# When the sums' rows and the products enter the sync queue: a change to a fused attention and gated-MLP kernel

## The chip, the cores and the metric

The kernel runs on one core of a Trainium2 chip. The core has a matrix engine (TensorE, PE in the rows; its weight loads are PEld), a vector engine (VectorE, DVE), a scalar engine (ScalarE, ACT), a general engine (GpSimd, POOL) and a sync engine (SyncE, SP), which here only issues transfers. Each engine runs its own instructions in the order in which they stand, and engines wait for each other by semaphores. Sixteen DMA engines move the data. The metric is the device time of one execution in microseconds; lower is better.

## The reference

Attention with an added relative bias, then a gated layer on the heads' joined outputs:

```python
scores = q @ k.T / 8 + bias            # 4 batches, 8 heads, 576 x 576, head size 64
attn   = exp(scores - max); attn = attn / (sum(attn) + 1e-9)
x      = (attn @ v) joined over heads  # 2304 tokens x 512
out    = (sigmoid(x @ w_gate) * (x @ w_val)) @ w_out     # 512 -> 1536 -> 512
```

The bias comes from a small two-layer net on log-distances and is the same for all batches.

## The kernel before, in words

**Stages.** The bias stage runs to about 111 us of the profiled span, attention from there to about 374 us, the gated layer from there to the end.

**Attention** (`attention`, lines 500 to 792) works through 16 units; a unit is one pair of heads of one batch. `n` counts slots, nine to a unit; slot `s` of unit `u` is `n = 9u + s`. Eight slots are blocks of 128 queries of one of the two heads (`TURN` gives head `h` and block `it`), the ninth holds the last 64 queries of both. In the even slots `score` (L633, L622) writes scores of two blocks to PSUM banks of the pool `ps_s`, and `soft` takes the row minimum on VectorE (L649) and the exponential on ScalarE (L654) to the tile `en`, with the row's sum. Two slots later (`LAG`) `turn` transposes the block for the second product and splits it into two half-precision parts in the tile `at`: half of the blocks on TensorE (L678, L685, then L563 and L564), the other half, the **crossed tiles** of turn slots 1, 3, 5 and 7 (`CROSS`; all of the second head, blocks 0 to 3), on GpSimd (L531, L672, tile `cr`) and then by one transposing DMA from `cr` to `at` (L673). These four DMAs of a unit are called **T1, T3, T5 and T7** here. They are put on the list `crossed` with the slot in which they are due, two after the turn: slot 5, slot 7, and slots 0 and 2 of the next unit.

**The second product** (`products`, L729) of unit `u - 1` runs in slots 3, 5, 7 of unit `u` and slot 1 of unit `u + 1`, 14 matmuls each time. Its first half (`e = 0`, slots 3 and 5) covers the first 288 queries, so it reads what T1, T3 and T5 bring; the second (`e = 1`) reads what T5 and T7 bring. Each half leaves the one accumulator bank (`ps_v`) by a ScalarE copy to `xe` (L733). After the second one, `xe` is written to memory (`xs`, L735).

**The sums.** At slot 3 `tail` of the unit before transposes its last 64 queries and its sums' inverses (`normal`, L698); in slot 4 ScalarE copies those to `rt` (L702), and two small DMAs write them to the rows `rs` (L704, L705).

**The order on the sync queue** is that of the code: within a slot first `after`, then `due` (loads of k, q and v for later units: `kr` L542 due at slot 2, `qr` L548 at slot 5, `vr` L553 at slot 1), then `softs` and `late` (here the `rs` rows), then the due crossed tiles, then the matmuls of `products` (here `xs`, in slot 1), then `extra`. A DMA that must wait for its data holds up all that stand behind it on the queue. The load `qr` waits until GpSimd has read the q before it (`prep_q`, slot 4), `kr` likewise (`prep_k`, slot 1).

**From unit 12 on** `extra` also starts the gated layer: by the table `PLAN` it loads parts of x (`xin`, L879), the sums' rows (`xrec`, L886) and weights (`ww`, L905), and scales and splits x (L894 to L896). `xin` tiles have three buffers, so a load of one can wait for the split (L896) of an earlier x. After the last unit the gated layer's first matmuls follow on TensorE (L974).

The lines below are the heart of the order; the functions that the change touches are printed after them.

```python
            for f in after:
                f()
            for f in due:
                f()
            for f in softs + late:
                f()
            due, loads = loads, []
            while crossed and (crossed[0][0] <= n or n == 9 * NU + LAG):
                crossed.pop(0)[1]()
```

Of the kernel before, what the change touches and what calls it, by code (L numbers as in the profile page):

```python
# [10 lines left out]
F32 = mybir.dt.float32  # L11
# [7 lines left out]
B, H, S, D = 4, 8, 576, 64  # L19
# [9 lines left out]
LAG, WSTEP, VSTEP, TAIL = 2, 2, (3, 5), 3  # L29
# [487 lines left out]
def attention(tc, att, q, k, v, biases, biasL, ident, xs, rs, sizes, extra):  # L517
# [3 lines left out]
    nc = tc.nc  # L521
# [48 lines left out]
    def prep_k(u):  # L570
        kt[u] = t = two.tile([128, 2, S], F32R, name="k")
        pool_split(t[:, 0], t[:, 1], qkraw[u, "kr"])
# [24 lines left out]
    ps_v = pool("ps_v", 1, space=PSUM)  # L597
    ps_s = pool("ps_s", 2, space=PSUM)
# [14 lines left out]
    def score(n):  # L613
        u, s = divmod(n, 9)
        ks, qs = kt[u], qt[u]
        if s == 0:
            state[u] = [st.tile([128, 9], F32, name="sm"), None, {}]
        if s == 8:
            ps = ps_s.tile([128, 2, 512], F32, name="sc")
            for i, (l, r) in enumerate(TERMS):  # L620
                for e in range(2):
                    nc.tensor.matmul(out=ps[:, e, 0:HF], lhsT=qs[:, l, 512:640], rhs=ks[:, r, HF * e:HF * e + HF],  # L622
                                     start=(i == 0), stop=(i == len(TERMS) - 1))
            return [soft(u, s, ps)]
        if s % 2:
            return []
        it = TURN[s][1]
        pair = [ps_s.tile([128, 2, 512], F32, name="sc") for _ in range(2)]
        for i, (l, r) in enumerate(TERMS):
            for e in range(2):  # L630
                for h in range(2):
                    rows = slice(64 * h, 64 * h + 64)
                    nc.tensor.matmul(out=pair[h][:, e, 0:HF], lhsT=qs[rows, l, 128 * it:128 * it + 128], rhs=ks[rows, r, HF * e:HF * e + HF],  # L633
                                     start=(i == 0), stop=(i == len(TERMS) - 1))
        return [soft(u, s + h, pair[h]) for h in range(2)]
# [22 lines left out]
    def turn(n):  # L658

        u, s = divmod(n, 9)  # L660
        p, b = units[u]
        if s == 0:
            state[u][1] = atp.tile([128, 2, 9, S], F16, name="at")
        sm, at, ens = state[u]
        h, it = TURN[s] if s < 8 else (0, 4)
        en = ens[4 * h + it if s < 8 else 8]
        i = slice(128 * it, 128 * it + 128)
        if s in CROSS:
            t = crp.tile([128, 2 * S], F16, name="cr")
            copy(t[:, 0:S], en)  # L670
            for a, z in ((640, slice(0, 512)), (S, slice(512, S))):
                nc.gpsimd.tensor_tensor(out=t[:, a:a + z.stop - z.start], in0=en[:, z], in1=t[:, z], op=ALU.subtract)  # L672
            crossed.append((n + LAG + XLAG, lambda: nc.sync.dma_start_transpose(out=at[:, h, :, i], in_=t)))  # L673
            return []
        after = []
        pt = ps_t.tile([128, 4, 128], F32, name="pt")
        for J in range(4):
            nc.tensor.transpose(pt[:, J], en[:, 128 * J:128 * J + 128], ident)  # L678
        if s == 8:
            return [split(at[:, h, 0:4, 512:576], at[:, h, 5:9, 512:576], pt[:, :, 64 * h:64 * h + 64]) for h in range(2)]  # L680
        after.append(split(at[:, h, 0:4, i], at[:, h, 5:9, i], pt))
        if it == 3:
            pt = ps_t.tile([128, 4, 128], F32, name="pt")
            for e in range(4):
                nc.tensor.transpose(pt[0:64, e], ens[4 * h + e][:, 512:576], ident)  # L685
            after.append(split(at[0:64, h, 4, 0:512], at[64:128, h, 4, 0:512], pt[0:64].rearrange("p e i -> p (e i)")))
        return after

    def tail(u):
        sm, at, ens = state[u]  # L690
        pt = ps_t.tile([128, 4, 128], F32, name="pt")
        nc.tensor.transpose(pt[0:64, 0], ens[8][:, 512:576], ident)
        last = normal(u, pt)
        return [split(at[0:64, :, 4, 512:576], at[64:128, :, 4, 512:576], pt[0:64, 0].rearrange("p (h i) -> p h i", h=2)), last]

    def normal(u, pt):
        p, b = units[u]
        nc.tensor.transpose(pt[0:9, 2], state[u][0], ident)  # L698
        rt = rtp.tile([9, 128], F32, name="rt")

        def leave():
            nc.scalar.activation(out=rt, in_=pt[0:9, 2], func=AF.Copy, scale=sizes["out"][0:9])  # L702
            to = rs[2 * p:2 * p + 2, S * b:S * b + S]
            nc.sync.dma_start(out=to[:, 0:512].rearrange("h (i p) -> h i p", p=128), in_=rt[0:8])  # L704
            nc.sync.dma_start(out=to[:, 512:576].rearrange("(o h) p -> o h p", o=1), in_=rt[8:9].rearrange("o (h p) -> o h p", h=2))  # L705

        return leave

    def invert(u):
        sm = state[u][0]  # L710

        def both():
            nc.vector.tensor_tensor(out=sm, in0=sm, in1=sizes["tiny"], op=ALU.add)
            nc.vector.reciprocal(out=sm, in_=sm)

        return both

    def products(u):
        p, b = units[u]
        sm, at, ens = state[u]  # L720
        vv = vsplit[u]
        xe = xep.tile([128, S], F32, name="xe")
        for e in range(2):
            cs = slice(HF * e, HF * e + HF)
            acc = ps_v.tile([128, 512], F32, name="acc")
            mms = [(J, z, 5 * y + J) for J in range(4) for z, y in TERMS] + [(4, z, 4) for z in range(2)]
            for i, (J, z, y) in enumerate(mms):
                for h in range(2):
                    nc.tensor.matmul(out=acc[D * h:D * h + D, 0:HF], lhsT=vv[:, h, J, z], rhs=at[:, h, y, cs],  # L729
                                     start=(i == 0), stop=(i == len(mms) - 1))  # L730

                def leave(cs=cs, acc=acc, e=e):
                    nc.scalar.activation(out=xe[:, cs], in_=acc[:, 0:HF], func=AF.Copy)  # L733
                    if e == 1:
                        nc.sync.dma_start(out=xs[128 * p:128 * p + 128, S * b:S * b + S], in_=xe)  # L735

                yield leave if i == len(mms) - 1 else None

    NU = len(units)
    crossed = []  # L740
    with tc.manual_schedule():
        work = iter(())
        after, late, due, loads = [], [], [], []
        for n in range(9 * NU + LAG + 1):
            u, s = divmod(n, 9)
            softs = score(n) if n < 9 * NU else []
            inverse = invert(u - 1) if s == 0 and u > 0 else None
            later = turn(n - LAG) if LAG <= n < 9 * NU + LAG else []
            if s == TAIL and u > 0 or n == 9 * NU + LAG:
                later += tail(u - 1)  # L750
            if s == KSTEP and u + 1 < NU:
                prep_k(u + 1)
                if u + 2 < NU:
                    loads.append(lambda z=u + 2: load_k(z))
            if s == QSTEP and u + 1 < NU:
                prep_q(u + 1)
                if u + 2 < NU:
                    loads.append(lambda z=u + 2: load_q(z))
            for f in after:
                f()  # L760
            for f in due:
                f()
            for f in softs + late:
                f()
            due, loads = loads, []
            while crossed and (crossed[0][0] <= n or n == 9 * NU + LAG):
                crossed.pop(0)[1]()
            after, late = ([], later) if s % 2 else (later, [])
            if inverse:
                inverse()  # L770
            if s == WSTEP and 0 < u < NU:
                work = products(u - 1)
            if n == 9 * NU + LAG - 1:
                work = products(u - 1)
            for _ in range(FILL[s] if n < 9 * NU else 14 if n < 9 * NU + LAG else 0):
                f = next(work, None)
                if f:
                    f()
            if s in VSTEP and u < NU:
                upper_v(u, VSTEP.index(s))  # L780
            if s - 2 in VSTEP and u < NU:
                after.append(lower_v(u, VSTEP.index(s - 2)))
            if s == 8 and u + 1 < NU:
                loads.append(lambda z=u + 1: load_v(z))
            extra(n)
        for f in after + late:
            f()
        for f in work:
            if f:
                f()  # L790


class Moe:
# [551 lines left out]
```

## Time and profile before

| what | value |
|---|---|
| runs | 789.0 us median of 3 (788.83 to 792.26) |
| the profiled execution | 791.89 us, of which the span from first to last instruction 790.1 |
| granted TensorE clock, mean | 0.982 of full speed |
| TensorE busy | 735.1 us, 93% |
| VectorE busy | 631.6 us, 80% |
| ScalarE busy | 549.6 us, 70% |
| GpSimd busy | 326.3 us, 41% |
| data moved by DMA | 112.43 MB, mean 142 GB/s |

Busy time is a sum over the whole span and hides that stages differ, so the stages are read one by one. In the rows "idle before, releaser" tells how long an engine stood still and what ended that; a transfer is named by out<-in (`at<-cr` is a crossed tile's transposing DMA). The sync engine's rows (SPq) are issues: their length is the time in which the queue is taken, not the transfer's.

### The profile page before, as it was taken

What the parts mean: (1) busy time and instruction counts of PE and PEld (TensorE: products, weight loads), DVE (VectorE), ACT (ScalarE), POOL (GpSimd) and SP (SyncE); (2) the same over time, 40 slices, a digit from 0 to 9 for tenths busy, and PEclk for the clock granted to TensorE, in tenths of its full rate; (3) what the DMA queues carried; (4) which work ended last, traced back from release to release, by engine and by line L of the source; (5) the groups of instructions that cost most, each with busy time, mean ns of one, the idle gap of its engine ahead of it and who ended that gap; (6) DMA issues with size and microseconds to landing.
All of it is one profiled execution on the core that took longest, in us unless ns stands there. A gap on an engine that the chain in (4) does not pass through costs nothing.

```text
span 790.1 us, 17816 instructions
## 1 busy us (share of the span) xinstructions
PE 735.1 (93%) x6695; PEld 537.6 (68%) x6695; DVE 631.6 (80%) x1342; ACT 549.6 (70%) x1190; POOL 326.3 (41%) x416
## 2 busy tenths in 40 slices
PE   7999979998989997787999999998999999999997
PEld 4888866776667775565999899964555555555553
DVE  6787889988888886983498988879988886777762
ACT  5887739788788886884676656676667667666653
POOL 2244349988888896750000000023533321544200
PEclk9999989999999998997999999999999999999999
DMA  6487315897886899676887742335412212422102
GB/s 201 142 212 172 124 59 110 183 180 138 167 186 144 185 185 210 143 162 161 289 271 237 246 140 91 129 111 180 146 62 81 81 54 74 152 69 80 54 1 80
DMA packets 130965, 112.43 MB, mean 142 GB/s; under 512 B 81216, under 2 KB 101824, under 8 KB 130880
## 3 DMA queue, kind: packets, MB, share of 16 engines
q1 hardware_dynamic: 126848, 105.74, 49.9%
q0 software_dynamic: 2112, 2.62, 2.2%
q10 hardware_dynamic: 1920, 2.95, 1.1%
q8 instruction: 52, 0.85, 0.5%
q14 instruction: 33, 0.27, 0.1%
HBM read 76.08 MB, written 18.95 MB: 120 GB/s over the span
## 4 chain that ended last, share of the span: by engine, by line
PE 53%; DMA 11%; ACT 7%; DVE 5%; POOL 5%; issue 3%; SPq 1%; ACTq 0%; POOLq 0%; DVEq 0%
PE po L998 16%; PE pg L1146 10%; DMA at<-cr 8%; PE pu L1146 7%; PE pg L974 6%; PE pu L974 6%; PE acc L729 4%; ACT en L654 3%; POOL cr L672 2%; PE sc L633 2%; ACT at L563 2%; PE pt L678 2%; POOL cr L531 1%; DMA wo<-scratch 1%; DVE wv L1115 1%
## 5 line engine op out<-in xcount | busy, mean ns | idle before, releaser
L1104 POOL TENSOR_TENSOR ws<-wm 128x256 f32<-128x256 f32 x44 | 44.3, 1006 | 296.5 <-DMA xt<-xs 158.7
L1146 PEld LDWEIGHTS <-wv 128*128 128x128 f16 x1008 | 98.1, 98 | 83.2 <-issue 8.2
L654 ACT ACTIVATE en<-en,mn 128x576 f32<-128x576 f32 x144 | 110.7, 773 | 18.5 <-DVE mn L649 17.1
L1146 PE MATMUL pg<-xq,wv 128*128 128x384 f16 x576 | 109.3, 326 | 2.6 <-ACT c L1172 2.2
L649 DVE CUSTOM_DVE_ANT_0 en<-sc,bias 128x576 f32<-128x576 f32 x128 | 91.8, 754 | 23.4 <-PE sc L633 21.1
L672 POOL TENSOR_TENSOR cr<-en,cr 128x512 f16<-128x512 f32 (+1 forms) x128 | 93.0, 748 | 5.4
L729 PE MATMUL acc<-at,vv 128*64 128x288 f16 x896 | 77.0, 304 | 16.4 <-DMA at<-cr 13.7
L998 PE MATMUL po<-wo,gh 128*128 128x512 f16 x288 | 85.6, 379 | 0.0
L1146 PE MATMUL pu<-xq,wv 128*128 128x384 f16 x432 | 82.0, 326 | 1.1 <-DVE c L1152 1.1
L564 DVE SCALAR_TENSOR_TENSOR at<-pt,at 128x512 f16<-128x512 f32 (+3 forms) x128 | 70.1, 568 | 13.3 <-ACT at L563 11.9
L633 PE MATMUL sc<-k,part 64*128 64x288 f32 x768 | 76.3, 318 | 3.3 <-DVE bias L443 1.8
L729 PEld LDWEIGHTS <-vv 128*64 128x64 f16 x896 | 52.1, 115 | 34.9 <-issue 25.4
L563 ACT ACTIVATE at<-pt 128x512 f16<-128x512 f32 (+3 forms) x128 | 60.3, 496 | 20.3 <-PE pt L678 20.1
L1152 DVE TENSOR_TENSOR c<-pu,c 128x384 f32<-128x384 f32 x72 | 40.0, 555 | 41.2 <-PE pu L1146 27.9
L633 PEld LDWEIGHTS sc<-k,part 64*128 64x128 f32 x768 | 59.4, 191 | 18.6 <-issue 10.4
L427 PE MATMUL bps<-cfs,ind 128*128 128x64 bf16 x1458 | 67.5, 193 | 3.3 <-DVE bias L443 1.8
L408 ACT ACTIVATE ind<-y 128x576 bf16<-128x576 f32 x100 | 62.4, 652 | 10.6 <-PE y L403 7.8
L427 PEld LDWEIGHTS <-ind 128*128 128x128 bf16 x1458 | 58.7, 98 | 9.4 <-issue 2.8
L678 PE MATMUL pt<-ident,en 128*128 128x128 f32 x320 | 52.5, 287 | 11.0 <-ACT en L654 5.5
L1164 ACT ACTIVATE gh<-c 128x384 f16<-128x384 f32 x48 | 25.1, 522 | 53.8 <-DVE c L1162 52.3
L531 POOL TENSOR_SCALAR cr<-en 128x576 f16<-128x576 f32 x64 | 43.0, 672 | 39.3 <-ACT en L654 30.8
L974 PE MATMUL pg<-xhi,w 128*128 128x384 f32 x192 | 54.0, 339 | 1.2 <-ACT g L983 1.2
(177 smaller groups left out, 1675.0 us busy)
## 6 DMA issues: line engine op xcount, KB each, us to landing
wm<-scratch SPq DMA_DIRECT2D x48, 256.0 KB
scratch<-wm SPq DMA_DIRECT2D x27, 256.0 KB
wo<-scratch SPq DMA_DIRECT2D x24, 256.0 KB
qr<-in_q_dram SPq DMA_DIRECT2D x16, 320.0 KB
vr<-in_v_dram SPq DMA_DIRECT2D x16, 320.0 KB
kr<-in_k_dram SPq DMA_DIRECT2D x16, 288.0 KB
xs<-xe SPq DMA_DIRECT2D x16, 288.0 KB
xrec<-rs SPq DMA_DIRECT2D x48, 96.0 KB
```

Of the source, the lines that this page charges most:

```text
L427: nc.tensor.matmul(out=o, lhsT=st, rhs=cfs[:, part], start=(part == 0), stop=(part == 2))
L563: nc.scalar.activation(out=hi, in_=ps, func=AF.Copy, scale=float(2.0 ** UP))
L564: return lambda: nc.vector.scalar_tensor_tensor(out=lo, in0=ps, scalar=float(2.0 ** UP), in1=hi, op0=ALU.mult, op1=ALU.subtract)
L633: nc.tensor.matmul(out=pair[h][:, e, 0:HF], lhsT=qs[rows, l, 128 * it:128 * it + 128], rhs=ks[rows, r, HF * e:HF * e + HF], start=(i == 0) ...
L649: nc.vector.tensor_tensor_reduce(out=half(en), in0=ps[:, :, 0:HF], in1=half(nbias), scale=-0.125, scalar=3.0e38, op0=ALU.add, op1=ALU.min, ...
L654: nc.scalar.activation(out=en, in_=en, func=AF.Exp, bias=mn, scale=-1.0, accum_out=sm)
L672: nc.gpsimd.tensor_tensor(out=t[:, a:a + z.stop - z.start], in0=en[:, z], in1=t[:, z], op=ALU.subtract)
L678: nc.tensor.transpose(pt[:, J], en[:, 128 * J:128 * J + 128], ident)
L729: nc.tensor.matmul(out=acc[D * h:D * h + D, 0:HF], lhsT=vv[:, h, J, z], rhs=at[:, h, y, cs], start=(i == 0), stop=(i == len(mms) - 1))
L974: self.nc.tensor.matmul(out=(pg, pu)[z], lhsT=l, rhs=r, start=(kc == 0 and i == 0), stop=(kc == 3 and i == 2))
L998: self.nc.tensor.matmul(out=po, lhsT=l[:, tt], rhs=r, start=(first and i == 0), stop=(last and i == 2))
L1146: nc.tensor.matmul(out=p, lhsT=W[i][:, l, at + kc], rhs=V[b][:, r, kc], start=(new and n == 0), stop=(n == 5), skip_group_check=not new)
```

## The change

It does four things. The writes of `rs` no longer go on the queue in slot 4, where `rt` is made: they are put on a new list `sends`, which is emptied once in each slot, and `send` puts itself back on it twice, so that they go out in slot 7 (two slots after the first chance, slot 5). The write of `xs` goes out one slot later, in slot 2. Within a slot the due crossed tiles come first, then `sends` and `due`. And for the last unit alone, the second half of the product accumulates in a bank of the score pool instead of the one bank of `ps_v`, so it does not wait for the first half's copy.

```diff
         def leave():
             nc.scalar.activation(out=rt, in_=pt[0:9, 2], func=AF.Copy, scale=sizes["out"][0:9])
+            sends.append(lambda: send(2))
+
+        def send(more):
+            if more:
+                sends.append(lambda: send(more - 1))
+                return
             to = rs[2 * p:2 * p + 2, S * b:S * b + S]
             nc.sync.dma_start(out=to[:, 0:512].rearrange("h (i p) -> h i p", p=128), in_=rt[0:8])
...
-            acc = ps_v.tile([128, 512], F32, name="acc")
+            if u == NU - 1 and e == 1:
+                acc = ps_s.tile([128, 2, 512], F32, name="sc")[:, 0]
+            else:
+                acc = ps_v.tile([128, 512], F32, name="acc")
...
                     if e == 1:
-                        nc.sync.dma_start(out=xs[128 * p:128 * p + 128, S * b:S * b + S], in_=xe)
+                        sends.append(lambda: nc.sync.dma_start(out=xs[128 * p:128 * p + 128, S * b:S * b + S], in_=xe))
...
-    crossed = []
+    crossed, sends = [], []
...
-            for f in due:
+            while crossed and (crossed[0][0] <= n or n == 9 * NU + LAG):
+                crossed.pop(0)[1]()
+            for f in [sends.pop(0) for _ in range(len(sends))] + due:
                 f()
             for f in softs + late:
                 f()
             due, loads = loads, []
-            while crossed and (crossed[0][0] <= n or n == 9 * NU + LAG):
-                crossed.pop(0)[1]()
...
         for f in work:
             if f:
                 f()
+        while sends:
+            sends.pop(0)()
```

On the engines that compute the order stays as it was, but for one x split on VectorE (L896) that moves behind a pair of score minima in unit 13. What moves stands on the sync queue.

The sync queue in a unit of the middle (units 3 to 11 are alike), from the T7 of the unit before, as it was:

```order
L673 DMA_TRANSPOSE at<-cr 128x9x128
L704 DMA rs<-rt 2x4x128
L705 DMA rs<-rt 2x1x64
L548 DMA qr<-in_q_dram 128x640
L673 DMA_TRANSPOSE at<-cr 128x9x128 x3
L553 DMA vr<-in_v_dram 128x640
L735 DMA xs<-xe 128x576
L542 DMA kr<-in_k_dram 128x576
```

and as it is now, from the same T7 on:

```order
L673 DMA_TRANSPOSE at<-cr 128x9x128
L744 DMA xs<-xe 128x576
L542 DMA kr<-in_k_dram 128x576
L673 DMA_TRANSPOSE at<-cr 128x9x128
L548 DMA qr<-in_q_dram 128x640
L673 DMA_TRANSPOSE at<-cr 128x9x128
L710 DMA rs<-rt 2x4x128
L711 DMA rs<-rt 2x1x64
L673 DMA_TRANSPOSE at<-cr 128x9x128
L553 DMA vr<-in_v_dram 128x640
```

T1, T3 and T5 stood together behind the two `rs` writes; now T1 stands behind `kr`, T3 behind `qr`, and T5 alone behind `rs`. T7 stood behind `xs` and `kr`; now these stand behind it.

The same queue in unit 12, where the gated layer's first loads come in, from T7 of unit 11 to T5 of unit 12, as it was:

```order
L673 DMA_TRANSPOSE at_6066<-cr_6269 128x9x128
L879 DMA xin_6362<-xs_57 128x384
L905 DMA ww_6364<-scratch_59 128x512
L704 DMA rs_58<-rt_6373 2x4x128
L705 DMA rs_58<-rt_6373 2x1x64
L879 DMA xin_6430<-xs_57 128x384
L905 DMA ww_6432<-scratch_59 128x512
L886 DMA xrec_6436<-rs_58 64x384 x2
L548 DMA qr_6444<-in_q_dram 128x640
L673 DMA_TRANSPOSE at_6329<-cr_6366 128x9x128
L886 DMA xrec_6465<-rs_58 64x384 x2
L673 DMA_TRANSPOSE at_6329<-cr_6439 128x9x128
```

and as it is now, from `kr` (which follows T7 and `xs`) on:

```order
L542 DMA kr_6337<-in_k_dram 128x576
L890 DMA xin_6362<-xs_57 128x384
L916 DMA ww_6364<-scratch_59 128x512
L890 DMA xin_6428<-xs_57 128x384
L916 DMA ww_6430<-scratch_59 128x512
L897 DMA xrec_6434<-rs_58 64x384 x2
L673 DMA_TRANSPOSE at_6328<-cr_6366 128x9x128
L548 DMA qr_6443<-in_q_dram 128x640
L897 DMA xrec_6463<-rs_58 64x384 x2
L673 DMA_TRANSPOSE at_6328<-cr_6437 128x9x128
L710 DMA rs_58<-rt_6373 2x4x128
L711 DMA rs_58<-rt_6373 2x1x64
```

Behind both pieces stand one more `xin` and then T5. T7 and the two `rs` writes are out of the way of the first loads; the `rs` writes are behind T3, ahead of T5, as in the other units.

The end of attention, the queue from the last early `xin` (part L2 of `PLAN`) through the last unit's four crossed tiles, as it was:

```order
L879 DMA xin<-xs 128x384
L673 DMA_TRANSPOSE at<-cr 128x9x128 x3
L735 DMA xs<-xe 128x576
L905 DMA ww<-scratch 128x512
L673 DMA_TRANSPOSE at<-cr 128x9x128
```

and as it is now:

```order
L890 DMA xin<-xs 128x384
L673 DMA_TRANSPOSE at<-cr 128x9x128 x2
L710 DMA rs<-rt 2x4x128
L711 DMA rs<-rt 2x1x64
L673 DMA_TRANSPOSE at<-cr 128x9x128
L916 DMA ww<-scratch 128x512
L744 DMA xs<-xe 128x576
L673 DMA_TRANSPOSE at<-cr 128x9x128
```

Here the `rs` writes, which stood ahead of that `xin`, come between T3 and T5; `xs` and `ww` stand between T5 and T7 both times.

## Rows read from the trace of the kernel before

**Rows 1.** Busy time by stage (stretch, length, busy per engine, clock, DMA share, GB/s).

```profile
138.00:298.30 160.30, 146.56 (x1521) 112.34 (x1520) 139.86 (x375) 133.87 (x342) 140.12 (x178) 1.00 0.85 171
374.44:518.15 143.71, 143.22 (x752) 132.97 (x753) 119.53 (x238) 92.26 (x206) 3.10 (x4) 1.00 0.60 198
```

**Rows 2.** What TensorE waited for, 138 to 298.3 us: total, times, longest.

```profile
PE acc L729 <- DMA at<-cr: 6.3, 9, 1.3
PE pt L678 <- ACT en L654: 4.1, 11, 0.5
```

**Rows 3.** One whole unit in the same view as rows 1.

```profile
269.80:284.03 14.23, 13.49 (x141) 10.36 (x140) 13.07 (x38) 12.53 (x34) 12.67 (x17) 1.00 0.94 173
```

**Rows 4.** SP's timeline in unit 6 (start, length, instruction).

```profile
209.54 0.63 SPq L704 DMA_DIRECT2D rs<-rt  x1
...
211.35 5.57 SPq L673 DMA_TRANSPOSE at<-cr  x3
...
218.14 0.33 SPq L735 DMA_DIRECT2D xs<-xe  x1
```

**Rows 5.** POOL's timeline in the same unit: crossed tiles 1, 5 and 7.

```profile
203.28 1.43 POOL L672 TENSOR_TENSOR cr<-en,cr 128x512 f16<-128x512 f32 x2
...
210.11 1.43 POOL L672 TENSOR_TENSOR cr<-en,cr 128x512 f16<-128x512 f32 x2
...
213.12 1.44 POOL L672 TENSOR_TENSOR cr<-en,cr 128x512 f16<-128x512 f32 x2
```

**Rows 6.** The chain that ended last, in unit 6 (start, length, what).

```profile
214.74 4.74 DMA at<-cr
```

**Rows 7.** TensorE's timeline in unit 6, slot 3 of the next one.

```profile
218.17 0.28 PE L729 MATMUL acc<-at,vv 128*64 128x288 f16 x1
219.61 1.02 PE L729 MATMUL acc<-at,vv 128*64 128x288 f16 x13 [1.16 <-DMA at<-cr]
```

**Rows 8.** The DMA engines just before rows 4's T1, view of rows 1.

```profile
208.00:211.30 3.30, 3.13 (x35) 2.31 (x34) 3.17 (x12) 3.30 (x9) 3.05 (x5) 1.00 0.01 3
```

**Rows 9.** TensorE's timeline after unit 12.

```profile
305.40 0.28 PE L729 MATMUL acc<-at,vv 128*64 128x288 f16 x1
308.87 1.89 PE L729 MATMUL acc<-at,vv 128*64 128x288 f16 x13 [3.19 <-DMA at<-cr]
```

**Rows 10.** The stretch behind that wait, view of rows 1.

```profile
308.80:314.60 5.80, 5.73 (x39) 4.15 (x41) 1.88 (x6) 1.59 (x3) 2.83 (x4) 0.50 1.16 227
```

**Rows 11.** SP's timeline in unit 12: T7 of unit 11, first ww, first rs.

```profile
291.95 1.30 SPq L673 DMA_TRANSPOSE at<-cr  x1
...
293.92 0.44 SPq L905 DMA_DIRECT2D ww<-scratch  x1
296.23 0.63 SPq L704 DMA_DIRECT2D rs<-rt  x1
```

**Rows 12.** The chain that ended last, T5 of unit 12.

```profile
305.09 3.73 DMA at<-cr
```

**Rows 13.** Waits of ACT and PE in unit 14, 336.4 to 352.4 us.

```profile
ACT vv L603 <- DMA vr<-in_v_dram: 1.3, 1, 1.3
...
PE pt L678 <- ACT rt L702: 1.0, 1, 1.0
```

**Rows 14.** DVE's timeline at the end of attention: the split of x.

```profile
351.88 0.93 DVE L896 TENSOR_TENSOR xlo<-xin,xhi 128x384 fp32r<-128x384 f32 x1
```

**Rows 15.** SP's timeline there: xin, T1, T5.

```profile
352.85 0.34 SPq L879 DMA_DIRECT2D xin<-xs  x1
...
353.30 1.63 SPq L673 DMA_TRANSPOSE at<-cr  x1
...
356.64 1.35 SPq L673 DMA_TRANSPOSE at<-cr  x1
```

**Rows 16.** TensorE's timeline there: the last unit's first half.

```profile
360.11 3.54 PE L729 MATMUL acc<-at,vv 128*64 128x288 f16 x27 [3.50 <-DMA at<-cr]
```

**Rows 17.** The chain that ended last, T7 of the last unit.

```profile
359.25 5.84 DMA at<-cr
```

## The prediction, made before the changed kernel ran

> **What bounds the kernel now.** I read the stages first, then TensorE's waits in attention, then the sync queue and the engines beside the longest of them. In the eleven middle units TensorE is the busiest engine, 146.56 of 160.30 us [rows 1], and in the gated layer it is busy 143.22 of 143.71 us (the second of [rows 1]): there nothing can be gained, but nothing is lost either, so that a shorter attention shortens the whole by as much. Of the 13.7 us that TensorE is idle in the middle units, 6.3 us in 9 waits end with the landing of a crossed tile's transposing DMA; the next cause, transposes that wait for the exponential, has 4.1 us [rows 2].
>
> Why these DMAs are late is seen in unit 6. T1's data are ready on GpSimd at 204.71 (203.28 + 1.43), T5's at 211.54 and T7's at 214.56 [rows 5]. But the queue stands at the `rs` write until 209.54, and T1 goes out at 211.35 [rows 4]; the DMA engines meanwhile are idle, 0.01 of the stretch 208.0 to 211.3 [rows 8]. T1, T3 and T5 then go out together, T5 at 214.74, and 4.74 us later TensorE is released [rows 6], after a wait of 1.16 us for T5 at the first half of the product [rows 7]. So here the place on the queue is late, 3.2 us behind the data (214.74 - 211.54), and neither the data nor the DMA engines. T7 goes out behind `xs`, which waits for ScalarE until 218.14 [rows 4], 3.6 us behind its data; it is read in slot 7, and the first middle units' waits are there.
>
> **The change part by part.**
>
> *The middle units.* Nothing that computes is added, so the cost is in queue places only. T1 and T3 no longer wait for `rt`; T5 stands behind T3 and the two `rs` writes, whose `rt` is copied three slots earlier (before 209.54), so it goes out when its data are there, near 211.6. With the 4.74 us of [rows 6] it lands at 216.4; TensorE needs it at 218.45, the end of the first matmul of its pair [rows 7]. Margin 2 us. T7 goes out near 214.6 instead of after 218.14 and has four slots left. All 6.3 us of [rows 2] go: 160.30 - 6.3 = 154.0, or 14.0 us a unit. Is there something behind it that holds the unit longer? A unit that had no such wait took 14.23 us, with TensorE busy 13.49, VectorE 13.07, GpSimd 12.67 and ScalarE 12.53 [rows 3]. So 14.0 to 14.2 is what the other waits allow, and I take **-6.3 us**; at 14.23 for all it is 160.30 - 156.5 = 3.8.
>
> *Moved DMAs that cost nothing.* `xs` stands behind T7 now, whose data are ready 3.6 us before `xe` is [rows 4, 5], so `xs` and the `kr` behind it keep their time; cover gone, `kr` has eight slots until GpSimd wants it. `qr` stands behind T1, whose data come a slot before its own wait for GpSimd ends. `vr` goes out sooner, as T5 does. The `rs` writes are three slots later, their readers at least a unit away until the last units, and `rt` has two buffers. One wait is new: in unit 14 a load of x (l3 of the plan) stands right behind the `xs` that it reads, and must wait for it to land. The longest landing here is 5.84 us [rows 17]; behind it is T1, due three slots (4.7 us) later and read some seven slots after that. No cost.
>
> *Unit 12.* The largest single wait is 3.19 us for T5 [rows 9], and the stretch behind it runs at a granted clock of 0.50 [rows 10], the 1.2 GHz level, after TensorE had stood still. The 5.73 us busy there would be half at 2.4 GHz: 2.87 us. T5 went out at 305.09 [rows 12]. Of the queue ahead of it two things go: the wait between `ww`'s end (294.36) and the `rs` write (296.23), 1.87 us, and T7's issue of 1.30 us [rows 11]. So T5 goes out near 301.9 and lands after 3.73 us [rows 12] at 305.6, after 4.74 [rows 6] at 306.6. TensorE asks for it at 305.68 (305.40 + 0.28) [rows 9]. A wait of 0 to 0.9 stays; the middle units had waits of up to 1.3 us [rows 2] at a clock of 1.00 [rows 1], so I let the clock stay up, and take 0.4. 3.19 + 2.87 - 0.4 = **-5.6 us**; from 3.2 (the wait alone) to 6.1.
>
> *Unit 14.* ScalarE waits 1.3 us for `vr`, and a TensorE transpose then 1.0 us for ScalarE's `rt` copy [rows 13]. `vr` goes out sooner as T5 does. **-1.0**; from 0 to 1.0.
>
> *The end of attention* gets worse. The queue is held by the `xin` load, which waits for VectorE's split of x, done at 352.81 [rows 14]; T1 goes out at 353.30 and T5 at 356.64 [rows 15]. That load still stands ahead of T1, so T1's time stays, while the two `rs` writes, 0.63 us [rows 4] and the like, with their gaps 1.35 together, now come between T3 and T5. T5 goes out at 358.0, TensorE waits 4.85 us instead of 3.50 [rows 16], and T7, behind the same `ww` and `xs`, moves as much: 360.6 instead of 359.25, landing 5.84 us later [rows 17]. It is T7's landing that starts the last half and ends the stage. **+1.35**. If the clock stays low longer for it, up to +2.7; if the `xin` load were done early, T5 could go out when its data are there (about 353) and the end would gain up to 3.6.
>
> A price from the Trainium skill, *DMA: Bandwidth & Descriptors*, section "Anatomy of one DMA": about 2.0 us plus the bytes over 436 GB/s, measured for the other issuing path. For a crossed tile of 295 KB it is an estimate of 2.7 us, by which T5 would land at 360.7 and the end would lose 0.6 of a microsecond; the trace shows landings of 3.73 to 5.84 us, and the sum goes by these.
>
> *The score bank* for the last half: 0. It saves a wait for the copy of the first half, but the last half waits for T7 beyond that, and with T7 later all the more. The bank itself was last read slots before.
>
> **Sum.** -6.3 - 5.6 - 1.0 + 1.35 = -11.55 us. The profiled execution took 791.89 us, so it would take 780.3. It is 2.9 us above the median of the runs, 789.0, within their spread; I put the sum on the median: **777.5 us**. Bounds: -6.3 - 6.1 - 1.0 - 3.6 = -17.0 (772.0) and -3.8 - 3.2 + 2.7 = -4.3 (784.7).
>
> **Rivals.**
>
> *The wait is handed on.* TensorE no longer waits for T5, but then for the exponential or the transposes' buffers: 4.1 us of such waits are there already [rows 2]. For: all four engines are busy over 12 of some 14 us. Against: the unit without a landing wait still took 14.23 [rows 3]. Half of the 6.3 is lost: -8.4, 780.6 us.
>
> *Unit 12 keeps its wait.* The first loads of the gated layer (`xin`, `ww`, `xrec`) stay ahead of T1, T3 and T5 there. For: they are over half of that queue's issues, and the margin worked out above is nil. Against: the 1.87 us wait and T7's issue are gone from it. Sum without that term and without unit 14's: -4.95, 784.0 us.
>
> *The end gains.* T1 is not held by the `xin` load, T5 goes out with its data: -16.5, 772.5 us.
>
> *The sixteen DMA engines are the bound.* Their share is 0.85 over the middle units [rows 1]. If they are full whenever it matters, an earlier issue only lands after a longer time. T5 may take 218.45 - 211.6 = 6.85 us to land before TensorE waits at all, and 8.0 before it waits as long as now. At 8.0 in the middle units and unit 12, only the end's 1.35 stays: 790.4, no change that can be told. Beyond 8.0 the kernel is slower by the excess once a unit: at 9.0, 12 x 1.0 + 1.35 = 13.4, 802.4 us. Against: no row shows over 5.84, the engines stand idle while the queue is held [rows 8], and the three tiles that now go out at once share the engines. A rule of the Trainium skill says as much as this rival: *DMA: Bandwidth & Descriptors*, "Issuing engines are not separate DMA queues", has all transfers run on the same sixteen engines and interleave there. By that rule spreading the issues wins nothing where the engines are full; the idle stretch of the trace speaks against its deciding here.
>
> *A part that does nothing.* That the score bank wins no time at the end is part of the forecast, not a case of its own.
>
> **How the numbers follow.** A measurement here can tell about 0.5% from no change, 3.9 us, so "faster" is below 785.1 and "slower" above 792.9. Chances: the forecast 0.64, the wait handed on 0.13, unit 12 keeps its wait 0.10, the end gains 0.04, the DMA engines 0.09, of which 0.03 slower. Faster: 0.64 + 0.13 + 0.04 and 0.07 of unit 12's 0.10 (its time is near the limit) = 0.88. Same: 0.06 + 0.03 = 0.09. Slower 0.03. The range runs from the forecast's lower bound, 772.0, to its upper one, 784.7, and takes in the first three rivals.
>
> **What would show it.** In the changed profile the waits of `acc` for `at<-cr` in the middle units should be near 0 and the units near 14.0 us; T1's issue within a microsecond or so of its GpSimd rows or of `kr`; no clock of 0.50 behind unit 12; the wait before the last unit's first half near 4.9 us. Landings over 6 us, or TensorE waits that moved to the exponential in the same amount, would make it wrong.

## The result, and the profile after

The changed kernel takes 780.35 us (median of 4 runs, 777.87 to 781.96) beside 790.17 us for the kernel before on the same chip: a ratio of 0.9871 with a 95% interval of 0.9832 to 0.991, faster by 9.8 us. The forecast was 777.5 us with a range of 772.0 to 784.7. The profiled execution took 779.37 us, of which 777.6 are span, 12.5 less than the profiled one before (790.1). That one lay 1.7 us above its median and this one 1.0 below, so a sum over the two profiles, as made here, gives 2.7 us more than the medians do. The forecast put its sum on 789.0; against 790.17 the same 11.55 us give 778.6.

The stages of the profile after, which answer to [rows 1] (stretch and length, then busy time and count of PE, PEld, DVE, ACT, POOL, then granted clock, DMA share, GB/s). In order: units 1 to 11, unit 12, unit 13, unit 14, the end of attention, the rest of the gated layer.

```profile
137.53:288.82 151.29, 144.61 (x1521) 112.56 (x1520) 140.47 (x375) 133.26 (x342) 139.85 (x180) 1.00 0.87 183
288.82:304.94 16.12, 13.44 (x141) 10.48 (x139) 13.71 (x38) 12.73 (x34) 14.34 (x18) 1.00 0.95 205
304.94:322.84 17.90, 14.50 (x141) 10.61 (x140) 17.26 (x42) 14.96 (x37) 13.56 (x17) 0.95 0.81 180
322.84:337.35 14.51, 13.76 (x142) 10.83 (x140) 12.41 (x34) 11.89 (x32) 8.03 (x11) 0.95 0.61 146
337.35:360.54 23.19, 14.72 (x118) 11.73 (x116) 10.46 (x24) 12.26 (x29) 2.63 (x7) 0.85 0.69 152
360.54:777.60 417.06, 407.74 (x2210) 278.10 (x2210) 325.87 (x566) 263.99 (x538) 85.51 (x88) 0.99 0.37 125
```

Of the kernel before, the same view of units 12, 13, 14 and the end, which [rows 1] do not hold:

```profile
298.30:319.10 20.80, 16.09 (x140) 11.86 (x140) 14.31 (x36) 12.20 (x32) 14.19 (x18) 0.84 0.86 185
319.10:336.43 17.33, 14.16 (x138) 10.48 (x139) 16.69 (x41) 14.72 (x37) 13.49 (x16) 0.96 0.73 154
336.43:352.31 15.88, 14.14 (x142) 10.97 (x140) 13.58 (x37) 12.12 (x32) 8.03 (x11) 0.94 0.81 175
352.31:374.44 22.13, 16.45 (x117) 13.21 (x116) 9.88 (x21) 12.15 (x29) 2.95 (x7) 0.77 0.65 160
```

| stretch | before | after | change | forecast |
|---|---|---|---|---|
| unit 0 and all ahead of it (to the first mark) | 138.00 | 137.53 | -0.5 | 0 |
| units 1 to 11 | 160.30 | 151.29 | -9.0 | -6.3 |
| unit 12 | 20.80 | 16.12 | -4.7 | -5.6 |
| unit 13 | 17.33 | 17.90 | +0.6 | 0 |
| unit 14 | 15.88 | 14.51 | -1.4 | -1.0 |
| end of attention | 22.13 | 23.19 | +1.06 | +1.35 |
| gated layer from there | 415.66 | 417.06 | +1.4 | 0 |
| sum | 790.1 | 777.6 | -12.5 | -11.55 |

The marks between the stretches are the first score matmul of each unit's last 64 queries (slot 8), so "unit 12" runs from slot 8 of unit 12 to slot 8 of unit 13. The end of attention runs on to the first gate matmul that waits for ScalarE's `g` (374.44 before, 360.54 after), so it also holds the gate matmuls ahead of that one, from 368.58 and 353.72 on, and the wait for `g`.

All causes of TensorE waits in units 1 to 11 of the kernel after, which answer to [rows 2]:

```profile
PE pt L678 <- ACT en L654: 3.5, 11, 0.3
PE pt L678 <- DVE at L564: 1.5, 9, 0.2
PE pt L678 <- ACT rt L702: 0.2, 1, 0.2
```

There is no row of `acc` for a transposing DMA any more, and the wait for the exponential has not grown (4.1 us before). Why can be read from the sync queue in unit 6 (start, length), beside [rows 4]:

```profile
205.53 1.27 SPq L673 DMA_TRANSPOSE at<-cr  x1
206.89 0.63 SPq L710 DMA_DIRECT2D rs<-rt  x1
...
208.25 1.34 SPq L673 DMA_TRANSPOSE at<-cr  x1
...
211.29 1.29 SPq L673 DMA_TRANSPOSE at<-cr  x1
```

and from GpSimd in the same stretch, which finishes the data of T3, T5 and T7 there (beside [rows 5]):

```profile
204.07 1.43 POOL L672 TENSOR_TENSOR cr<-en,cr 128x512 f16<-128x512 f32 x2
...
206.22 1.44 POOL L672 TENSOR_TENSOR cr<-en,cr 128x512 f16<-128x512 f32 x2
...
208.38 1.43 POOL L672 TENSOR_TENSOR cr<-en,cr 128x512 f16<-128x512 f32 x2
```

T3 goes out 0.03 us behind its data (205.50), T5 0.59 us behind (207.66) where it was 3.2, and T7 1.48 us behind (209.81) where it was 4.4, for in the kernel before T7 stood behind `xs` and `kr`:

```profile
218.99 1.67 SPq L673 DMA_TRANSPOSE at<-cr  x1
```

The queue follows the data. The DMA engines' share is 0.87 where it was 0.85, and no landing is waited for any more, so the rival that makes them the bound is out.

### The profile page after: what moved, and what is told of

The parts are those of the page before. It is cut to its first block, busy times and chain, and to the rows that moved or that the text cites. A ratio compares the mean times of both kernels' runs of the same rounds, so it can differ in the third digit from the quotient of the medians.

```text
span 777.6 us, 17819 instructions
## 1 busy us (share of the span) xinstructions
PE 729.3 (94%) x6695; PEld 536.0 (69%) x6695; DVE 632.7 (81%) x1342; ACT 549.0 (71%) x1190; POOL 325.3 (42%) x416
## 4 chain that ended last, share of the span: by engine, by line
PE 59%; DVE 11%; ACT 9%; issue 4%; DMA 2%; POOL 0%; SPq 0%; ACTq 0%; DVEq 0%
PE po L1009 16%; PE pg L1157 10%; PE pu L1157 7%; PE pg L985 6%; PE pu L985 6%; PE acc L738 5%; PE sc L633 4%; PE pt L678 3%; DVE en L649 3%; ACT at L563 3%; ACT en L654 3%; DVE at L564 2%; PE sc L622 1%; DVE wv L1126 1%; DVE xt L1041 1%
## 5 line engine op out<-in xcount | busy, mean ns | idle before, releaser
L738 PE MATMUL acc<-at,vv 128*64 128x288 f16 x868 | 68.8, 296 | 9.0 <-DMA at<-cr 6.2
L738 PEld LDWEIGHTS <-vv 128*64 128x64 f16 x896 | 49.8, 112 | 24.7 <-issue 20.7
L1009 PE MATMUL po<-wo,gl 128*128 128x512 f16 x144 | 54.6, 379 | 0.0
```

Of the source, the lines that this page charges most:

```text
L1009: self.nc.tensor.matmul(out=po, lhsT=l[:, tt], rhs=r, start=(first and i == 0), stop=(last and i == 2))
```

## The experiments

All eight start from the changed kernel. The first four ran beside a kernel before of 791.11 us, the other four beside one of 789.51, so kernels are compared by their ratio to the kernel before; stretches are of one profiled execution each.

**The `xs` write back in its old slot.**

```
-                        sends.append(lambda: nc.sync.dma_start(out=xs[...], in_=xe))
+                        nc.sync.dma_start(out=xs[...], in_=xe)
```

> The change, with one part undone: the write of xs goes out in slot 1 again, ahead of T7; kr stays behind T7. Theory (the rs writes ahead of T1, T3 and T5 were the larger part of the waits, T7 has slack): the eleven middle units take 151.3 to 154.3 us in all (151.3 with the whole change, 160.3 before), TensorE waits at most 0.3 us a unit for T7 at slot 7, and the run is 0 to 3 us slower than the change. Rival (T7 behind xs was the larger part): the middle units go back to 156 us or more, and the run is 5 us or more slower than the change.

782.08 us, ratio 0.9887 (0.9862 to 0.9912), which cannot be told from the change's 0.9871. Units 1 to 11 are as in the change; unit 12 is longer, 18.88 us:

```profile
137.22:288.35 151.13, 144.54 (x1522) 112.47 (x1520) 140.22 (x376) 133.30 (x342) 139.65 (x180) 1.00 0.84 181
```

So moving `xs` wins nothing in the middle. In unit 12 the wait for T5 is 3.15 us in this profile, 1.55 in the change's; but the kernel without the score bank (below), with the change's own queue, has 2.01 there, so at most part of it is due to `xs`, and the two times do not separate.

**The `rs` writes back in the slot of their copy.**

```
-            sends.append(lambda: send(2))
+            send(0)
```

> The change, with the other part undone: the two rs writes go out in slot 4 as before, ahead of T1, T3 and T5; xs stays behind T7. Theory: T5 goes out as late after rs as before, so the waits for it at slot 3 come back, 0.7 to 1.3 us in most units: middle units 157 to 162 us (151.3 with the change), unit 12's wait near 3 us with the half clock behind it, and the wait before the last unit's first half near 3.5 us instead of 4.7. In all 7 to 12 us slower than the change. Rival: the middle units stay below 154 us.

789.87 us, ratio 0.9982 (0.9966 to 0.9998): nearly the whole gain is gone. Units 1 to 11, and the waits of TensorE for landings there, which are back (unit 12 takes 21.44 us):

```profile
138.15:295.21 157.06, 145.76 (x1521) 112.34 (x1520) 139.99 (x375) 133.58 (x342) 139.00 (x177) 1.00 0.77 175
```

```profile
PE acc L738 <- DMA at<-cr: 4.6, 5, 1.5
```

Two writes of 4 and 0.5 KB, on the queue before their data exist, cost most of what the change brings. Both kernels send the same bytes, so the place on the queue is the cause: in unit 6 of this run the queue issues nothing from 203.11 to the `rs` write at 207.94. They came back with the crossed tiles still first in a slot and `xs` still late.

**The crossed tiles again last in a slot** (the `while crossed` loop back behind `due, loads = loads, []`).

```
-            while crossed and (...):
-                crossed.pop(0)[1]()
...
             due, loads = loads, []
+            while crossed and (...):
+                crossed.pop(0)[1]()
```

> The change, but within a slot the due crossed tiles come behind sends and loads, as before: T7 stands behind xs and kr again, T1 behind qr, T3 behind rs. Theory: T5 is as early as in the change, T7 as late as before: waits only at slot 7, 0 to 0.7 us a unit, middle units 151.3 to 158 us, the run 0 to 7 us slower than the change and more so than with xs early. Rival (the place within the slot is what counts): middle units near 160 us.

784.46 us, ratio 0.9908 (0.9882 to 0.9933): about 0.4% of the change's 1.3%, with intervals that overlap. In units 1 to 11 the landing waits are small, 1.0 us in three:

```profile
138.36:291.95 153.59, 145.31 (x1521) 112.47 (x1520) 140.10 (x378) 133.88 (x344) 139.37 (x177) 1.00 0.82 177
```

2.3 us of it are in the middle units (153.59 against 151.29), 2.7 in unit 12, where the wait for T5 is 2.67 us; of these, too, a part is what unit 12 varies by. So, each undone by itself, the early `rs` costs 5.8 of the 9.0 us that the change gains in the middle units (157.06 against 151.29), the place within a slot 2.3, and `xs` nothing.

**The `rs` writes two slots later still**, so that they stand behind T5.

```
-            sends.append(lambda: send(2))
+            sends.append(lambda: send(4))
```

> The change, with the rs writes two slots later still, behind T5. Theory: in the middle units nothing moves (T5 had slack), 151.3 us; in unit 12 T5 goes out 1.3 us sooner and the wait of 1.55 us for it falls to 0.2 to 0.5; at the end T5 and T7 go out 1.3 us sooner, the wait before the last unit's first half is 3.3 us instead of 4.7. In all 2 to 3 us faster than the change, about 778 us beside 780.35. Rival (the end is set by something else than the rs writes): the wait at the end stays near 4.7 us and the run is equal to the change.

777.42 us, ratio 0.9827 (0.9805 to 0.9848), some 3 us below the change by the medians, though the intervals touch. The middle stays (151.19). In unit 12 and at the end the waits for T5 fall from 1.55 to 0.58 and from 4.67 to 3.20 us:

```profile
298.02 1.02 PE L738 MATMUL acc<-at,vv 128*64 128x288 f16 x13 [0.58 <-DMA at<-cr]
...
346.19 3.34 PE L738 MATMUL acc<-at,vv 128*64 128x288 f16 x27 [3.20 <-DMA at<-cr]
```

The end's 1.47 us is what the two issues took there (0.65 + 0.60 and the gaps): the term of the sum that has T5 late by them is shown.

**Without the score bank for the last half.**

```
-            if u == NU - 1 and e == 1:
+            if u == NU and e == 1:
```

> The change without its last part: the last unit's second half of the product accumulates in the one bank of ps_v again. Theory: 0 us, because that half waits for T7 until after the first half's copy anyway (351.89 against a copy that ends at 350.78 in the changed kernel); the time is within 1 us of the change, and the wait before the second half is again for T7. Rival (the bank is part of the gain): 1 us or more slower, and a wait of that half for the copy.

779.43 us, ratio 0.9868 (0.9845 to 0.9891), where the change had 0.9871: the bank brings nothing. ScalarE copies the first half by 352.97, and TensorE's last half still waits for T7 after that:

```profile
354.10 1.84 PE L738 MATMUL acc<-at,vv 128*64 128x288 f16 x13 [0.68 <-DMA at<-cr]
```

This kernel has the change's sync queue in unit 12 and yet waited 2.01 us there, with a clock below full behind it (0.90 over the unit, 17.93 us long; the change 1.00 and 16.12). That difference of 1.8 us lies between two executions of one order of work.

**The `xin` load `L2` five slots later**, behind T1, T3 and T5 of the last unit.

```
-    ... 31: "x3 L2", ... 36: "s", ...
+    ... 31: "x3", ... 36: "s L2", ...
```

> The change, with the load of x for part L2 put behind T5 of the last unit (PLAN step 36 instead of 31). It tests the step that the load, which waits for VectorE's split of x, holds T1, and with the rs writes makes T5 late at the end. Theory: T1 goes out near 335 instead of 338.9, T5 near 338.4 instead of 343.45; the wait before the last unit's first half falls from 4.7 us to 0.3 to 1.0, T7 goes out near 342 instead of 346 and attention ends 3 to 4 us sooner; about 3.5 us faster than the change. Rival (the landing is slow there whatever the issue): the wait stays over 3 us.

773.45 us, ratio 0.9793 (0.9759 to 0.9827). By the ratios that is some 6 us below the change, where 3.5 were expected. The wait for T5 at the end is gone, and T7 is the next one. TensorE at the end, and the chain of waits to its last half:

```profile
339.04 1.91 PE L738 MATMUL acc<-at,vv 128*64 128x288 f16 x28
...
344.66 1.74 PE L738 MATMUL sc<-at,vv 128*64 128x288 f16 x18 [3.14 <-DMA at<-cr]
```

```profile
338.72 0.46 SPq L744
...
339.27 5.35 DMA at<-cr
```

The prediction said that this load sets T1's time at the end. With it moved, T1 goes out 5.4 us ahead of the mark that starts the end (329.25 and 334.61) instead of 1.6 behind it, and what sets T7's time is the `xs` write, which waits for its copy. The end takes 18.77 us, 4.4 less than in the change. That is more than half of the 8.3 us between the two profiles; 1.6 more lie in units 13 and 14 and 1.1 in the gated layer, where the change's TensorE ran at a lower clock. Behind unit 13's wait for `rt`, 2.3 us in both, the clock is 1.00 here to the unit's end and 0.62 in the change:

```profile
319.23:320.81 1.58, 1.58 (x19) 1.14 (x20) 1.58 (x4) 1.58 (x4) 1.50 (x2) 1.00 0.67 174
```

That part of the gain was not expected, and no run shows what this load has to do with it.

**Both together**, with the last `ww` load and `L2` in the plan's slot 38, behind T5 and the `rs` writes.

```
-            sends.append(lambda: send(2))
+            sends.append(lambda: send(4))
...
-    ... 31: "x3 L2", ... 36: "s", 37: "t X0"}
+    ... 31: "x3", ... 37: "t X0", 38: "s L2"}
```

> The version that should beat both: the rs writes two slots later, behind T5, and both the weight load and the load of x that stood ahead of T7 at the end are put behind T7. Theory: middle units 151.2 us, unit 12's wait near 0.6 us, T5 of the last unit out with its data (wait 0 to 0.5 us), T7 out near 342 and landing in 3.5 to 4.5 us instead of 5.9, so attention ends 5 to 6 us sooner than in the change; 5 to 7 us faster than the change, some 774 us where the change has 780. Rival (what is freed at the end is taken back by the gated layer's first loads, which now come later): no faster than with the rs writes alone later, some 777.

771.26 us, ratio 0.9766 (0.9736 to 0.9796): below both kernels, some 8 us below the change by the ratios where 5 to 7 were expected. It is the lowest median of the study, but its interval overlaps that of the load moved alone. Unit 12 has no wait for T5 left; at the end T7 is bound by the same `xs` write (339.43) and landed in 4.78 us:

```profile
289.58:304.48 14.90, 13.42 (x142) 10.47 (x140) 13.80 (x38) 12.61 (x34) 13.79 (x17) 1.00 0.97 225
```

```profile
339.87 4.78 DMA at<-cr
```

**The same without the score bank** (`u == NU` in its condition, as above).

> As the run before, but the last second half in the one bank of ps_v. With T7 landing sooner the copy of the first half may be what comes last. Theory: T7 still lands after the copy (some 345.5 against 344.6), so within 1 us of the run before. Rival: the second half waits 0.5 us or more for the copy, and the run is as much slower.

771.64 us, ratio 0.9778 (0.9746 to 0.981). With the T5 wait gone, the last half's start now does meet the copy, for 0.21 us, and the wait for T7 behind it is 2.27 us, so the bank stays without a measurable effect:

```profile
342.50 0.28 PE L738 MATMUL acc<-at,vv 128*64 128x288 f16 x1 [0.21 <-ACT xe L742]
```

## Why the prediction was right, point by point

**The middle units: mechanism right, -6.3 was too small.** The mis-sized term is "all 6.3 us of [rows 2] go": the waits went, but they had cost 9.0. The row of a wait counts from the modelled end of the matmul ahead of it, and undisturbed matmuls overlap that (one alone has a row of 0.28 us [rows 7], 14 in a run take 1.05). TensorE's rows of the kernel before, an undisturbed run of 14 and one that lost time without a wait row:

```profile
215.08 1.05 PE L729 MATMUL acc<-at,vv 128*64 128x288 f16 x14
...
282.61 1.45 PE L729 MATMUL acc<-at,vv 128*64 128x288 f16 x14
```

A run that is not disturbed takes 1.05 to 1.12 us. The one of [rows 7] took from 218.17 to 220.63, 2.46 us, so against the usual 1.07 it lost 1.39 where its row says 1.16. Over the nine waits, start of the first matmul to end of the last less 1.07 each, this comes to 8.5 us. Four more runs have no wait row but took 1.25, 1.30, 1.19 and 1.45 us (the last is shown): 0.9 more. Together 9.4, against 9.0 measured. The experiment with `rs` early agrees: 4.6 us of rows in 5 waits, 5.8 us lost (157.06 against 151.29). The other guess, that a unit could not be shorter than the 14.23 us of [rows 3], was wrong the other way: the units after are 13.75 us each, since that unit, with no listed landing wait, has the run of 1.45 in it.

**Unit 12: -4.7 for -5.6.** The step that failed is "T5 goes out near 301.9". Taken from the unit's mark, T5 went out at 6.79 us before (305.09) and was forecast at 3.6. After, it went out at 5.29 us. The sync queue of the kernel after, from the sums' rows for the gated layer on, and TensorE's wait:

```profile
284.93 2.35 SPq L897 DMA_DIRECT2D xrec<-rs  x2
287.39 1.36 SPq L673 DMA_TRANSPOSE at<-cr  x1
...
290.64 1.50 SPq L673 DMA_TRANSPOSE at<-cr  x1
...
294.11 1.61 SPq L673 DMA_TRANSPOSE at<-cr  x1
```

```profile
297.76 1.02 PE L738 MATMUL acc<-at,vv 128*64 128x288 f16 x13 [1.55 <-DMA at<-cr]
```

From `xrec` to T5 the queue issues one piece after the other with little between: its issue time is what binds, and it is longer than forecast. The two `xrec` issues took 2.35 us where they took 1.13 before; where they took 1.13 again, in the experiments with `rs` behind T5 and without the bank, T1 behind them took 2.83 and 3.20 instead of 1.36. T3 took 1.50 and T5 1.61 where 1.27 to 1.34 are usual in unit 6. With 1.35 us of issues moved behind T5, the wait fell to 0.58. Why an issue is sometimes longer is open; moving the `xrec` loads alone was not tried. "I let the clock stay up" held in this execution (1.00) and not in the four others with longer waits here (2.01, 2.67, 3.15 and 3.84 us: 0.84 to 0.91 over the unit). So the rival in which unit 12 keeps its wait was half right: the place is on the edge. Part of the stage's gain was not in the sum at all: at its end TensorE waited 0.71 us for VectorE's minima before, and not after, when the x split that used to stand ahead of those minima had moved behind them.

**Unit 14: -1.4 for -1.0.** As forecast, `vr` comes in time. With `rs` early again, unit 14 takes 17.72 us and TensorE waits for ScalarE's `vv` once more. That `xin` stands behind the `xs` it reads did wait, from 313.6 to 317.9, but TensorE waited for no landing in units 13 and 14.

**The end: +1.06 for +1.35, near by luck.** The rows that answer to [rows 15 to 17], the sync queue and TensorE:

```profile
338.49 0.33 SPq L890 DMA_DIRECT2D xin<-xs  x1
338.92 3.06 SPq L673 DMA_TRANSPOSE at<-cr  x2
...
343.45 1.29 SPq L673 DMA_TRANSPOSE at<-cr  x1
...
345.98 2.42 SPq L673 DMA_TRANSPOSE at<-cr  x1
```

```profile
346.77 3.52 PE L738 MATMUL acc<-at,vv 128*64 128x288 f16 x27 [4.67 <-DMA at<-cr]
...
351.89 1.90 PE L738 MATMUL sc<-at,vv 128*64 128x288 f16 x27 [0.65 <-DMA at<-cr]
...
360.54 0.44 PE L985 MATMUL pg<-xhi,w 128*128 128x384 f32 x1 [2.38 <-ACT g L994]
```

(The wait here, 3.50 us before, was the longest in attention, not the 3.19 of unit 12 as the prediction had it.) On the queue the prediction held. T5 goes out 4.96 us behind `xin`, before 3.79, and the wait is 4.67 us instead of 3.50. T7 moved by 1.09 against `xin` (7.49 from 6.40), and TensorE starts on it 5.91 us later (5.88 before). With `xin` itself 0.60 us later behind the mark, which the sum did not have, the last half starts 1.7 us later (14.54 us behind the mark, 12.82 before).

The step that failed is "It is T7's landing that starts the last half and ends the stage". The stretch from the last half's start to the first gate matmul, before and after:

```profile
365.13:368.58 3.45, 3.45 (x27) 2.90 (x27) 1.03 (x3) 2.69 (x8) 0.00 (x0) 0.50 0.12 21
351.89:353.72 1.83, 1.83 (x28) 1.50 (x28) 0.28 (x1) 1.44 (x6) 0.00 (x0) 1.00 0.17 63
```

The granted clock had come back by then, so TensorE reached its first gate matmul only 0.1 us later (16.37 us behind the mark, 16.27 before). What ends the stage is the wait for ScalarE's `g`, 2.38 us long instead of 1.15:

```profile
374.44 0.44 PE L974 MATMUL pg<-xhi,w 128*128 128x384 f32 x1 [1.15 <-ACT g L983]
```

In the changed kernel the chain that ended last does not go through T7. It goes from ScalarE's copy of the first half, for which T5 decides, through ScalarE's and VectorE's further work to `g`:

```profile
350.37 0.41 ACT xe L742
...
360.11 0.39 ACT g L994
```

The kernel without the bank had the lower clock in its last half (0.51) and came to the gate matmuls 1.5 us later than the change (17.91 us behind the mark), and its stage still took 23.20 us beside 23.19. So 1.7 us of delay, 1.6 given back by the clock and a longer wait for `g` add up to a number near the forecast. T5 took 3.3 us to land. The price from the Trainium skill, *DMA: Bandwidth & Descriptors*, section "Anatomy of one DMA", from which an estimate of 2.7 us came and a loss of 0.6, is below every landing that these rows show; the measurements decide.

**What was not forecast.** The gated layer's +1.4 lies right behind that wait for `g`: its first 24 matmuls and their gaps, up to the first output matmul, took 5.86 us where they took 4.28 at a clock of 1.00 before.

```profile
360.54:366.40 5.86, 5.86 (x25) 5.86 (x26) 1.66 (x4) 3.86 (x10) 0.00 (x0) 0.71 0.79 266
```

The clock fell like this in one other kernel, with the crossed tiles last, behind a wait of 2.57 us for `g` (0.70); behind waits of 0.77 to 2.10 us in the others it stayed at 1.00. From the first gate matmul to the end of the span the kernels of this study take 421.2 to 424.8 us, longest in these two.

Unit 13's +0.6 has two parts. A transpose of TensorE waits 0.25 us for VectorE, where the x split that moved now stands in front, and comes 0.35 us later in the unit. And behind the wait of 2.3 us for `rt`, which is in both kernels, the clock to the unit's end was 0.62 where it was 0.69:

```profile
320.41:322.84 2.43, 2.43 (x20) 1.52 (x20) 2.40 (x7) 2.43 (x6) 1.90 (x3) 0.62 0.85 203
```

The sum was 11.55 and the profiles show 12.5, because the 2.7 us too little in the middle, with 1.2 in unit 0, unit 14 and the end, more than made up for 0.9 in unit 12 and 2.0 in unit 13 and the gated layer. That errors of both signs nearly cancel is luck; the mechanism in the middle units is not.

## What to carry to other kernels

On a queue that issues in order, a transfer of a few kilobytes that is queued before its data exist costs what stands behind it, so look for the wait at the head, and give each transfer the place where its data are ready. What a wait costs is read from a whole run of matmuls against an undisturbed run of the same kind, not from the wait's row alone. Once the heads are cleared, the next limit can be the queue's own issue time, as in unit 12: remove or delay loads that nobody needs yet from the unit that is short of queue time.

## What the runs showed that was not expected

- An idle row is shorter than the loss: 1.16 us in the row and 1.39 lost at the wait of [rows 7], and 8.5 lost for 6.3 in the rows over the nine waits.
- The issue of one transposing DMA held the sync queue from 1.25 to 2.66 us in the kernel before, with a median of 1.47; two in a row took 3.06 us at the end of the change and 4.33 in unit 6 with `rs` early. The queue, not the transfer, then sets the next one's start.
- The wait alone does not tell what the clock does: behind the same 2.3 us in unit 13 it was 0.62 in the change and 1.00 with the load moved.
- After the wait of 1.55 us in unit 12 the granted clock was 1.00 over the unit; after one of 2.01 us at the same place, in the kernel without the bank, it was 0.59 for the next 4.2 us, and TensorE was busy for 4.14 of them. The unit was 1.8 us longer for a wait that was 0.46 us longer.

```profile
298.65 1.18 PE L738 MATMUL acc<-at,vv 128*64 128x288 f16 x13 [2.01 <-DMA at<-cr]
```

```profile
298.60:302.80 4.20, 4.14 (x33) 3.09 (x34) 1.31 (x4) 0.71 (x2) 3.68 (x4) 0.59 0.95 300
```
